# One issue list, 130 of 2459 operations in another place: an S4D convolution and a linear attention on one core

## The chip, the cores and the metric

The kernel runs on one core of one Trainium2 chip. The metric is the device time of one execution in microseconds; three executions of the kernel before the change took 543.41, 543.82 and 544.84 us, median 543.82. Engine names as the profile has them: PE is TensorE (PEld its weight loads), DVE is VectorE, ACT is ScalarE, POOL is GpSimd, SP is the engine that here issues all DMAs (SPq its queue).

## The reference

Two independent halves, concatenated along the last axis; 2048 positions, 576 channels, all float32.

```python
def _A_ref(u, log_A_real, A_imag, C_real, C_imag, log_dt, D_skip):
    dt = jnp.exp(log_dt)
    A = -jnp.exp(log_A_real) + 1j * A_imag
    C = (C_real + 1j * C_imag) * dt[:, None]
    P = jnp.exp((A * dt[:, None])[:, :, None] * pos[None, None, :])   # 576 x 128 x 2048
    K = 2.0 * jnp.einsum("dn,dnl->dl", C, P).real
    y = irfft(rfft(u_t, 2L) * rfft(K, 2L), 2L)[:, :, :L]              # a causal convolution
    return y.transpose(0, 2, 1) + u * D_skip[None, None, :]

def _B_ref(x, wqkv, w_phi, wo):                                       # 32 heads of 18
    q, k, v = split(x @ wqkv)
    pq, pk = q @ w_phi, k @ w_phi                                     # per head
    phi_q = concat([softmax(pq), softmax(-pq)]); phi_k = the same of pk
    kv = einsum("bhsf,bhsd->bhfd", phi_k, v); z = phi_k summed over s
    o = (phi_q @ kv) / (phi_q @ z + 1e-6)
    return o.reshape(B, S, D) @ wo
```

## The kernel before

The convolution is done as a two-stage Fourier transform by matmuls. Its parts, by the names in the program: `u` (16 units, the first transform stage of the input, stored to DRAM), `par` and `mags` (the parameters: steps and magnitudes), `group` (18 units, each of which builds a piece of the long kernel K: phases on GpSimd in integers, a sine on ScalarE, a rotation by matmuls `g0`, ScalarE copies `g2` at L811, VectorE multiplications `g3` at L815 to L820, and a reduction by 64 small matmuls `g4`), `kfirst` (4 units, the first stage of the transform of K), `product` (16 units: load spectra `ff` and `ub`, matmuls `p1` and `p2`, the complex product, the inverse stage `p4`, a store), and `last` (16 units: load, `l1` a matmul with `w1`, a copy to `ot`, four stores to the output at L979). The attention has `fold` (weights of wqkv and w_phi multiplied), 16 `key` tiles of 128 positions (projection, two softmaxes, `k4`: the sum of phi_k times v), `kv`, and 16 `query` tiles (projection, softmaxes, product with kv, division, product with wo, a store at L589). Large matmuls go in two float32 halves (`vh`, `vl`, `wh`, `wl`).

All of it is made first as a list of 2459 operations numbered in the order in which the body calls them, and then issued in the order of one long string, `ORDER`. No scheduler runs: each engine has one queue in program order, and what is in front in the string is in front in its engine's queue. An operation starts when its queue has come to it and its semaphores are there. A word of `ORDER` is a number, with `x` for the other of two permitted engines, `@` and digits for the PSUM bank or banks of its result (8 banks), and `:n` for n zero matmuls put on TensorE ahead of it, written into the bank that the operation itself will write:

```python
            word, _, fill = word.partition(":")
            word, _, at = word.partition("@")
            k = int(word.rstrip("x"))
...
            for _ in range(fill):
                self.matmul(t[0:cols, 0:n], self.zero.t[0:rows, 0:cols], ...)
```

Buffers in SBUF belong to tags with a number of copies that are used in turn (`e`, `x9`, `ot` and `ac` have 3, `cs` and `ub` 5, `ff`, `zo`, `zi` 2, `small` 7), so an operation that writes a buffer also waits until the last user of that copy is done. SP issues its DMAs in the string's order; the ninth waits until the first has landed, and so on: eight are under way at most.

The operations that the prediction names:

| number | what it is | engine before |
|---|---|---|
| 298 | key tile 12: maximum minus e (softmax, L310) | VectorE |
| 278, 279 | key tile 11: minimum (L437), then its subtraction | VectorE, GpSimd |
| 80, 81 | key tile 1: maximum (L434), e minus it (L314) | VectorE |
| 1140, 1141, 1432 | par: phase arithmetic (L314, L734) | VectorE |
| 173, 174 | key tile 6: low half of x (L310) | VectorE, GpSimd |
| 303, 305 | key tile 12: clearing of v (L487); `k4` | GpSimd, TensorE |
| 386, 366, 396 | fold and kv: a copy of a weight, an output copy; a fold product | VectorE, VectorE, TensorE |
| 1034, 1035, 1036 | u 8: matmul, its two copies (L300) | TensorE, ScalarE, VectorE |
| 1444, 1470, 1520, 1519, 1943 | group: `g0` (1444, 1519, 1520, 1943), `g4` (1470) | TensorE |
| 463, 464, 465, 466 | query tile 1: minimum, subtraction, exponential, sum | VectorE, VectorE, ScalarE, GpSimd |
| 428 | query tile 0: e minus maximum | VectorE |
| 1540, 1543, 1546 | group 8: copy (L811), multiplication (L816), `g4` | ScalarE, VectorE, TensorE |
| 2305, 2263, 2221; 2278 | products 14, 12, 10: load of `ff`; product 12's `p4` | SP; TensorE |
| 2033, 2111 | products 1, 5: load of `ub` | SP |
| 2380, 2385, 2387, 2350, 2353 | last 4, 5, 5, 0, 0: output store (L979) | SP |
| 2424, 2431, 2438 | last 11, 12, 13: load (L966) | SP |
| 2432, 2439 | last 12, 13: `l1` | TensorE |
| 2434, 2443, 2449, 2455 | last 12, 13, 14, 15: output store (L979) | SP |
| 880, 917 | query tiles 12, 13: output store (L589) | SP |
| 773; 544, 1338, 1471, 1801 | query 10: low half of x; four copies out of PSUM | VectorE |
| 1932, 2014, 2020 | a copy, product 0's multiplication (L938), a copy | ScalarE, GpSimd, ScalarE |

Of the kernel before, what the change touches and what calls it, by code (L numbers as in the profile page):

```python
# [1000 lines left out]
113 114 84 1196 1018 1007 75 1038 1205 1230 1197 1198 211 1182 1179 280 1185 1186 281 1231 282 179@0 177@2 1142 176 116@6 117 325 115 175 1206 85 180
181 182 1207 1208 183x 86 1143 283x 286 1190@52 1232 1233 1234 120 121 87x 1187@3 1218 1189@67 1235 1237 1238 1239 326 122 1221 1188 178 327 1209 1404
212 189 1211 328x 123x 88 118@2 330@0 90 119 213x 124 1210 1212 1214 1213 1191@67 184 129 1215 185 1220 188 1240 1144 1241 1216@5 214 1242 216@2 215
1145 1146 1269 91 1243 128 1236 1223 186 306 1268 187x 1224 1219 1222 92 1217 93 1405 1270 1271 331@6 219 220 94 332 1100 329 221 222 125 190 126 1419
# [67 lines left out]
968 969 872@60 2418@2 2431 940@1 873 874 2448 2456 2457 2449 875 876 941 944 970 971@6 975@0 878@4 972 945 2419 942 946@17 2458 947 973@6 2451 2450  # L1072
877 879 976x 974x 948 2410 2455 2420 2422 2421 2423 2432@2 2439@0 2440 949 2403 2411@4 880 980@6 981 982 2424 950 2433 977@0 2444 951@2 978 2441 2436
979 983@10 2412 2442 984 2443 985 2437 986 2404@6 2435 2415 2434 2405x 2425@4 2426 2414 952 2416 2413 2409 2408 2407 2406 2428 2430 953 954 2427 2429
987 988@6 989 990 991
"""


# [16 lines left out]
```

## Time and profile before

| | |
|---|---|
| runs | 543.41, 543.82, 544.84 us |
| the profiled execution | 545.11 us, of which 543.3 us from the first to the last instruction |
| TensorE busy | 521.5 us (96%), granted clock 0.998 |
| VectorE, ScalarE, GpSimd busy | 455.9 (84%), 382.1 (70%), 328.8 (61%) us |
| DMA | 107.01 MB, mean 197 GB/s |
| zero matmuls | 118 |

In the timeline's rows stand the start, the length, the engine, the line, the operation, output and inputs and, in brackets, how long the engine had been idle ahead of it and what released it. Rows of neighbouring equal instructions are joined (x2, x64).

### The profile page before, as it was taken

How to read it: one execution, taken by the hardware profiler on the slowest of the kernel's cores; microseconds unless marked ns; L12 is line 12 of the kernel's file. 1: busy time of each engine (PE TensorE's matmuls, PEld its weight loads, DVE VectorE, ACT ScalarE, POOL GpSimd, SP SyncE). 2: the span in 40 equal slices, each digit the busy share in tenths (PEclk: the TensorE clock that was granted, in tenths of full speed). 3: DMA queues.
4: the chain of work that ended last, by engine and by line, in shares of the span. 5: the costliest groups of instructions: out<-in, count | busy, mean ns of one | idle time of the engine just before them, and what ended most of it. 6: DMA issues, size and time to landing. Idle time of an engine off the chain costs nothing.

```text
span 543.3 us, 19242 instructions
## 1 busy us (share of the span) xinstructions
PE 521.5 (96%) x8192; PEld 435.9 (80%) x8192; DVE 455.9 (84%) x716; ACT 382.1 (70%) x555; POOL 328.8 (61%) x456
## 2 busy tenths in 40 slices
PE   8999999999999989999999999999899999999995
PEld 7999899888888767888878666766689877776984
DVE  7999899898868889999989996999974889787641
ACT  4868798798559799889689977989733444343332
POOL 1173885958777775982758998997433617434300
PEclk9999999999999999999999999999999999999999
DMA  8936711244245678246664588756458789998785
GB/s 235 326 105 195 281 45 31 101 139 134 89 139 190 207 241 294 83 128 196 229 205 118 153 265 250 241 180 194 131 173 271 234 281 293 287 281 260 265 252 157
DMA packets 86163, 107.01 MB, mean 197 GB/s; under 512 B 5698, under 2 KB 70338, under 8 KB 86078
## 3 DMA queue, kind: packets, MB, share of 16 engines
q1 hardware_dynamic: 86078, 105.79, 61.5%
q8 instruction: 64, 1.05, 0.8%
q14 instruction: 21, 0.17, 0.1%
HBM read 61.22 MB, written 44.54 MB: 195 GB/s over the span
## 4 chain that ended last, share of the span: by engine, by line
PE 69%; DVE 13%; DMA 7%; ACT 4%; issue 3%; SPq 2%; POOL 1%; DVEq 0%; ACTq 0%; POOLq 0%
PE psum L295 63%; PE psum L549 3%; DMA ff<-in_ff_dram 2%; DMA dram<-zi 2%; PE psum L237 2%; DVE ac L314 1%; DVE cs L816 1%; SPq L979 1%; PE psum L577 1%; DMA cs<-dram 1%; DVE e L310 1%; DMA ub<-dram 1%; DVE e L314 1%; DVE small L434 1%; DVE small L437 1%
## 5 line engine op out<-in xcount | busy, mean ns | idle before, releaser
L295 PE MATMUL psum<-vh,x 128*128 128x288 f32 x576 | 123.6, 301 | 0.5 <-ACT ks L300 0.5
L295 PE MATMUL psum<-wh,x 128*128 128x288 f32 x576 | 124.1, 302 | 0.0
L757 POOL TENSOR_TENSOR cs<-cs,pi 128x32 int32<-128x32 int32 (+4 forms) x180 | 108.5, 608 | 8.0
L295 PEld LDWEIGHTS psum<-wh,x 128*128 128x128 f32 x576 | 94.1, 188 | 7.7 <-issue 4.2
L295 PEld LDWEIGHTS psum<-vh,x 128*128 128x128 f32 x576 | 94.0, 188 | 5.4 <-issue 3.2
L295 PE MATMUL psum<-vl,x 128*128 128x288 f32 x320 | 93.8, 295 | 0.0
L295 PE MATMUL psum<-wl,x 128*128 128x288 f32 x320 | 93.7, 295 | 0.0
L811 ACT ACTIVATE psum<-psum 128x512 f32<-128x512 f32 x108 | 59.9, 588 | 15.4 <-PE psum L295 14.9
L295 PEld LDWEIGHTS psum<-vl,x 128*128 128x128 f32 x320 | 60.2, 188 | 0.0
L295 PEld LDWEIGHTS psum<-wl,x 128*128 128x128 f32 x320 | 60.2, 188 | 0.0
L310 POOL TENSOR_TENSOR x<-zo,x 64x128 fp32r<-64x128 f32 (+1 forms) x30 | 25.4, 848 | 46.3 <-ACT x L394 35.1
L310 POOL TENSOR_TENSOR e<-e,small 128x1152 f32<-128x1152 f32 (+1 forms) x24 | 41.2, 1720 | 14.5 <-DVE small L450 7.8
L815 DVE TENSOR_TENSOR cs<-psum,cs 128x1024 f32<-128x1024 f32 x36 | 43.6, 1212 | 3.7 <-ACT psum L811 3.6
L310 POOL TENSOR_TENSOR e<-small,e 128x576 f32<-128x576 f32 x26 | 30.6, 1177 | 25.4 <-DVE small L437 23.6
L816 DVE TENSOR_TENSOR cs<-psum,cs 128x1024 f32<-128x1024 f32 x36 | 43.6, 1214 | 1.4 <-PE psum L295 1.3
L295 PE MATMUL psum<-ub,ff 64*32 64x288 f32 x1024 | 40.0, 410 | 4.3 <-DMA ff<-in_ff_dram 1.9
L295 PEld LDWEIGHTS psum<-kvb,fT 126*128 126x128 f32 (+1 forms) x320 | 38.3, 188 | 7.2 <-issue 2.9
L295 PEld LDWEIGHTS psum<-cs 128*32 128x32 f32 x2304 | 34.1, 110 | 11.2 <-issue 2.9
L295 PE MATMUL psum<-cs 128*32 128x64 f32 x2304 | 40.0, 220 | 2.6 <-DVE cs L816 0.9
L295 PE MATMUL psum<-kvb,fT 126*128 126x133 f32 (+1 forms) x320 | 41.6, 280 | 0.1
L440 ACT ACTIVATE e<-e 128x1152 f32<-128x1152 f32 x32 | 37.0, 1164 | 2.7 <-POOL e L310 1.3
L781 ACT ACTIVATE cs<-cs 128x1040 f32<-128x1040 int32 x36 | 38.3, 1064 | 0.6 <-POOL cs L776 0.4
(156 smaller groups left out, 1115.2 us busy)
## 6 DMA issues: line engine op xcount, KB each, us to landing
dram<-zi SPq DMA_DIRECT2D x32, 576.0 KB
ub<-dram SPq DMA_DIRECT2D x64, 288.0 KB
dram<-zo SPq DMA_DIRECT2D x32, 288.0 KB
zo<-in_xT_dram SPq DMA_DIRECT2D x24, 320.0 KB
zi<-dram SPq DMA_DIRECT2D x12, 576.0 KB
ub<-in_u_dram SPq DMA_DIRECT2D x16, 288.0 KB
xd<-x SPq DMA_DIRECT2D x8, 576.0 KB
x<-xd SPq DMA_DIRECT2D x8, 576.0 KB
```

The lines of the kernel that those rows point to most:

```text
L237: self.matmul(t[0:cols, 0:n], self.zero.t[0:rows, 0:cols], self.data.t[0:rows].bitcast(BF16)[:, 0:n], start=not o[13], stop=not o[13], ski ...
L295: pe.matmul(o, l, r, start=start, stop=stop, skip_group_check=skip)
L310: op(eng, [c_dve(n[0]) if e == "dve" else c_pool(n[1]) for e in eng], lambda e: (dve if e == "dve" else pool).tensor_tensor(dst(), a(), b( ...
L314: op(eng, c_dve(n) if eng == "dve" else c_pool(n), lambda: e.tensor_tensor(dst(), a(), b(), op=alu), r=r, w=w, with_=with_, lock=eng == "p ...
L434: op("dve", c_dve(D), lambda: dve.tensor_reduce(two(top.t), v(), axis=AX.X, op=ALU.max, negate=True), r=[p], w=[top])
L440: op("act", c_act(1152) + 40, lambda: act.activation(e.t, e.t, AF.Exp), r=[e], w=[e], table="exp")
L549: pe.transpose(tp.t[0:m, j - j0, :], e.t[:, sign, 7 * g:7 * g + GRP[g], :].rearrange("p h f -> p (h f)"), ident.t)
L757: op("pool", c_pool(2 * n * W), lambda n=n, j=j: pool.tensor_tensor(x()[:, :, :, n:2 * n], x()[:, :, :, 0:n], pi.t[:, j:j + 2, gs].bitcast ...
L781: act.activation(cs.t[:, 1], cs.t[:, 1].bitcast(I32), AF.Sin, scale=TURN)
L811: op("act", c_act(512), lambda b=b: act.activation(b.t, b.t, AF.Exp), r=[b], w=[b], table="exp")
L815: op("dve", c_dve(64 * W), lambda: dve.tensor_tensor(F(), both(M.t), F(), op=ALU.mult), r=[M, cs], w=[cs])
L816: op("dve", c_dve(64 * W), lambda: dve.tensor_tensor(E.t[:, :, :, 32:64], both(up.t), cs.t[:, :, :, 0:32], op=ALU.mult), r=[up, cs], w=[E])
```

## The change

Only the string `ORDER` differs. Buffers, operations and their arithmetic are the same. 130 operations stand in another place, nearly all a few words from where they were; 2033 and 2111 go back over fourteen and eight of SP's DMAs, 2424 forward over some fifteen, 2393 over ten, 853 back behind several of GpSimd's. Eleven change the engine: 298, 464 and 773 from VectorE to GpSimd; 544, 1338, 1471 and 1801 from VectorE to ScalarE; 1035, 1932 and 2020 from ScalarE to VectorE; 2014 from GpSimd to VectorE. Zero matmuls: 749, 792, 1044, 1520 and 2278 get two, 1444 and 1943 four, 1993 two in place of three. Some 20 operations write another PSUM bank. The parts of the string with the larger changes (words of `ORDER`, shortened to those places):

```diff
-1200 1163 293 273@6 272 357 66 67 73x 1159 1164 1160 1065 1088 298x 1089 50@4 299 358 1090 1168 74 1165 70 304 359 1166 1167 77@2 300 276 1139 1401
-301 277 1402 362 172 173x 1169 1170 1192 302 76 274@0 1140 275 80 278 1141 1403 1091 1148 1147 279 1149 1150 174 303 1193 1201 1151@56 1172 111 1098
+1200 1163 293 66 273@6 272 357 67 73x 360 1159 1164 1160 358 298 1065 1088 1089 50@4 299 1090 1168 74 1165 70 304 1166 1167 77@2 300 276 359 1139 1401
+301 277 1402 362 172 1169 1170 1192 1193 302 76 274@0 278 1403 1140 275 80 81 1141 173x 1091 1148 1147 279 1149 1150 174 303 1201 1151@56 111 1098
...
-1524 1525 1526 366 1036x 1529 1531 1532 386 1443@54 1527 1528 1533 1534 1462 1463 1009@06 1464 1035 1011 1444@23 403@6 1466 1467 402 1535 1445@54 1465
-1472 1010 406 1468 404 394 1473 1043 1537 387 458 1469 1470@2 1474 396@0 395 1536 399 408 1475 1037 405 407 1471x 1476 388@6 1478 1477 1361 1362 389
+1522 1523 1524 1525 386 1526 366 1036x 1529 1531 1532 1443@54 1527 1528 1533 1534 1462 1463 1009@06 1011 1464 1035x 1444@23:4 403@6 1466 1467 402 1535
+1445@54 1465 1472 1010 406 1468 404 394 1473 1043 1537 396@0 387 458 1469 1470@2 1474 395 1536 399 408 1475 1037 405 407 1471 1476 388@6 1478 1477
...
-994@62 398 995x 372x 996x 1012 415 459@0 364 365 1429 460 369x 374x 1430 373x 370x 375 1431 997 461 462 1432 426@6 425 1538 463 1376 416 417 1433
-1044@24 464x 1434 1435 1688 376 377 1520@01 427 428 1377 1519@67 1539 1046 1045x 155 1436 1541 429 526 465 492 418 1542 1014@24:8 430 1540 1545 1544
+371@5 368x 1013 994@62 398 995x 372x 1012 415 459@0 364 374x 365 996x 1429 460 369x 1430 373x 370x 375 1431 997 461 462 426@6 425 1538 463 1432 1376
+416 417 1433 1044@14:2 1434 464 1435 1688 376 377 427 428 1377 1519@67 1539 1046 1045x 1520@01:2 155 1436 1541 1540 429 526 465 492 418 1542 1014@42:8
...
+956 957x 958x 898 2229 858 767 902 843 2353 2322 2221 2323 2228 2277 924 2385 2350 2362@4 2226@0 2324 2352 925 926 2224@2 2363x 2232@4 2325 2396 768
...
-934@2 935 938@5 2241 963 2402 870 2401 2400 939 867 964 965 966 871 868 936@6 915 916 2445 2452 937x 2446@2 2447 2417 2453@4 967 2454x 2438 943@7 917
-968 969 872@60 2418@2 2431 940@1 873 874 2448 2456 2457 2449 875 876 941 944 970 971@6 975@0 878@4 972 945 2419 942 946@17 2458 947 973@6 2451 2450
-877 879 976x 974x 948 2410 2455 2420 2422 2421 2423 2432@2 2439@0 2440 949 2403 2411@4 880 980@6 981 982 2424 950 2433 977@0 2444 951@2 978 2441 2436
+2417 2453@4 967 2454x 2438 2424 943@7 917 968 969 872@60 2418@2 2431 940@1 873 2449 874 2448 2456 2457 875 876 941 944 970 971@6 975@0 878@4 972 945
+2419 942 946@17 2458 947 973@6 2451 2450 877 2455 879 976x 974x 948 2410 2439@0 2420 2422 2421 2423 2432@2 2440 949 2403 2411@4 880 2443 980@6 981 982
```

More of the change, by code (lines that the diff above doesn't have):

```diff
@@ L1001 @@
[L1001 to L1004, printed above, removed]
@@ L1073 @@
[L1073 to L1075 removed]
+0 1 2 4 1104 3 1097 1093 68 1094 5 1096 1154 1105 1107 34 6 1092 1108 1109 51 1095 27 7@0:49 20 1106 1110 1111 1112 1113 1114 1115 8 35@2 1199 1137 11
+28@4 29 52 12 1116 1120 9 53x 30 36 10 54 13 22@6 32 37 1003 21 1117 39 992 1118 31 1119 40 15@0 14 1074 23 33 38 1121 1063 344 18 25 16 345 24
@@ new lines @@
+2000@6 2001 1844 1733 2123 1837 1810 588 589 2124@24 2125 2126 1845x 2002@6 2006@0 2008@4 1945 1846x 2003 2007 2009 2012 2010 2011 1818 624@6 2014x
+625 2127 1947 626x 1803@20 2130 1805x 1811@46 1847 1812x 1804 1813 2013 2015@20 636 2132 1826@6 2129 2138 2128 637 2137 2016 1827 1948 1949 2135@4
+2133@6 2090 1950 1952 1953 2017 1954 2018x 2136 2141@4 2022x 1955 2134 2020x 2142 2019 1956 2139@6 2021 525 1828@23 590@0 1848 2089 2140 1829@45 1849
+2095 1851 1852 1830@67 1850 1853 1957 1958 1951 591 663@2 2023 1959 1854 1857 1860 2144 1960x 638 2143 1855@4 592x 1858 664 1859 1915 639 1862 1961
@@ new lines @@
+2088 1914 1916 1863 1861 1917 665 666 667 2093@0 2091@6 2092 1856 1864@5 1814 2094 2096 2097@6 1918 640 1919 2024 696 1920 2099@2 697 1865x 627
+2145@04 2098 668 1907 1942@67 1962 2100 2075 1908 2146 2069 1963 643@2 669 698 1909 1943@34:4 1964 1965 641@5 642 645@6 699 1971 2147 700@0 2102 644
+1944@52 1966 1967 1968 1974 1910 1973 2101 1969@7 646 701 1806 1911 1972 1922 1970 670 1912 671 1913 1976 1921 2067 2148 2149 2068 1977 672 1975 593
+2150 2074 673 1877 674 2103@62 2104 702 1978@4 703 1876 2070@2 1870 1869 2033 2025 2072@0 647@5 2026 1878 2027 1979x 2071x 2073x 2105 2107 650@4 1923
@@ new lines @@
+706 707 810 2040@02 688 1930 1929 689 1941x 2200 690 691 1931@4 1932x 1980 1993@64:2 2041 773 2042 1995x 1994 1981@20 1989@64 1982x 2044 1983x 2043
+774@2 708 1996 775 1990 733 709 710 711x 776 734 735 736 777 1984 778 779 1991 692@0 1985@62 1987 811@4 714@2 2045 715 1986x 812 1992 813 712@3 1988
+844 713x 716@6 780 2368 2180 693 717 781 718@7 721@6 782 814 738@2 2369@4 719 694 722 720 783 784 2179 2175@0 881 2370 845 846 847 723 2183@6 2181@4
+737 2389 2176 724@01 815 816 2182 725 2184 726 727 739 2185 728 817 882 883x 849@4 848 785x 850 2207 661 730@6 786@0 787 851 2372 2201 695 884 2202
@@ new lines @@
+2373 2250 2186 852 729 790@1 731 2187 788@0 818 819 820 2208 2375 2189 2188 2374 789 2203@4 2371 791x 732 2205@6 2204 2390@0 2243 2206 2211@4 740
+2209@2 2212 2391 2190@60 2191 795@5 792@4:2 2307 2210 2192 821 2244 2193x 2196 822x 823@2:6 2194 2195 2242 2213x 2197 796 2249 2247@0 793 824 797 794
+2214x 2245@6 2376@2 2248 2246 2253@0 2347 2377 2251@4 2215@62 2198 2199 2254 2252 2393 741 2327 885@0 2216 798@23 742 2328 799 2217 2218x 825@4 827@5
+2326 800 801 826x 2333 886 2329@6 2334 828x 802 2219 887 2330 2394 2331@4 2332 743 2335@2 2337@6 2220 888 2382 2336 2256 2255 2257@04 889 2258 2285
@@ new lines @@
+832@2 744 890 829@3 2338 2286 803@4 2259 2339x 745 2284 833 830 834 2383@6 891 831 2384 2289@0 2392 2287@2 2260 2291 892 746 2290x 835@67 893 836 853
+837 2288 804 747 838 839 2261 2395 2340 2341@02 2292 2293@6 805 2295@4 748 2262 2342 2361 753@2 751@3 2343 2306 2380 2313 2296 752 841@0 2294 2305
+749@3:2 754x 2308@6 750 2381 2310@4 2309x 2312 2316@2 2311 2344 2314@6 2317 758@5 2345 2265 2378 2298 755@4 2297 2315 756 759 894 757 895 760 896x
+2346 2299@26 806 918 919 920x 761@45 762 840 921 2270 763 2264 899@4 2387 2379 2300 764 2319 2348@6 2301 2318 842 2263 2266@2 900x 2267 2268@0 765
@@ L1076 @@
+2407 2406 2428 2430 953 954 2427 2429 987 988@6 989 990 991
 """
```

119 lines of the change are left out of this document (51 added, 68 removed).

## The prediction

> **What bounds the kernel.** I read the page's busy times and its chain first, then busy time by stretch, then what TensorE waited for, then the timeline where a wait stood beside a moved operation.
>
> ```profile
> PE 521.5 (96%) x8192; PEld 435.9 (80%) x8192; DVE 455.9 (84%) x716; ACT 382.1 (70%) x555; POOL 328.8 (61%) x456
> ...
> PE 69%; DVE 13%; DMA 7%; ACT 4%; issue 3%; SPq 2%; POOL 1%; DVEq 0%; ACTq 0%; POOLq 0%
> ```
> ```profile
> 28.00:56.00 28.00, 27.30 (x329) 25.26 (x330) 27.85 (x39) 22.16 (x28) 15.38 (x24) 1.00 0.52 165
> ...
> 180.00:220.00 40.00, 35.72 (x599) 30.01 (x600) 34.24 (x61) 36.27 (x52) 27.70 (x41) 1.00 0.81 264
> ...
> 442.00:500.00 58.00, 56.00 (x920) 42.05 (x907) 46.54 (x71) 23.63 (x38) 28.30 (x21) 1.00 0.93 290
> 500.00:543.30 43.30, 37.33 (x406) 32.97 (x390) 18.37 (x40) 14.48 (x25) 6.14 (x5) 0.98 0.69 219
> ```
>
> TensorE is busy 521.5 of 543.3 us and nothing of its real work changes, so a reordering can only win what it stands idle, or lose by more of it. By stretch (columns: stretch, its length, then PE, PEld, DVE, ACT, POOL busy, clock, DMA share, GB/s) VectorE has no gap at 28 to 56, TensorE idles 4.3 us at 180 to 220 and 6.0 us in the tail, and the DMA engines are 93% busy at 442 to 500. So I price four places and a residue; elsewhere the moves mostly swap neighbours whose inputs are there in either order, and I put them at zero with the engines' queues as cover. If that cover is thin, the waits quoted below show what one slip costs: 0.25 to 1.2 us each.
>
> **Part 1, at 55 us: operation 298 (key tile 12's subtraction) goes from VectorE to GpSimd; 278 is put ahead of 1140 and 80, and 173 behind 1141.**
>
> ```profile
> 41.59 1.02 DVE L310 TENSOR_TENSOR e<-small,e 128x576 f32<-128x576 f32 x1
> ...
> 51.64 0.54 DVE L314 TENSOR_TENSOR pi<-pi,ot 128x384 f32<-128x384 f32 x1
> 52.10 0.74 DVE L434 TENSOR_REDUCE small<-psum 128x32 f32<-128x576 f32 x1
> 52.77 0.73 DVE L437 TENSOR_REDUCE small<-e 128x32 f32<-128x576 f32 x1
> ...
> 40.40 0.72 POOL L310 TENSOR_TENSOR x<-zo,x 64x128 fp32r<-64x128 f32 x1 [3.12 <-ACT x L394]
> ...
> 53.66 1.41 POOL L310 TENSOR_TENSOR e<-small,e 128x576 f32<-128x576 f32 x1 [8.76 <-DVE small L437]
> ...
> 55.66 0.16 POOL L487 MEMSET v<- 128x32 f32 x1
> ...
> 54.77 0.18 PEld L295 LDWEIGHTS psum<-sel,mg 64*128 64x128 f32 x1 [0.54 <-DVE e L314]
> 55.87 0.75 PE L295 MATMUL psum<-e,v 128*19 128x36 f32 x64 [0.60 <-POOL v L487]
> ```
>
> TensorE waits 0.54 us (81, VectorE, which also frees a bank) and 0.60 us (303, the GpSimd memset). GpSimd stood idle 8.76 us for 278 (the L437 row), then ran 279, 174 and 303 in a row. Without 298 VectorE is 1.02 us ahead; 278 also passes 0.54 + 0.74, so 279 starts some 2.5 us earlier and ends near 52.6. Then 174 needs 173, which now stands behind 1141: near 53.8; 303 follows at about 54.5. TensorE would come to its product at 55.87 - 0.60 - 0.54 = 54.7. Both waits go: 0.54 + 0.60 = 1.1 us. 298 itself fits in GpSimd's gap of 3.12 us ahead of 40.40. Late next would be 303 itself, with 0.2 us to spare; for 173 only 174 waits. Bounds: 0 (another wait takes over) to -1.1.
>
> **A rule on GpSimd against the rows.**
>
> ```profile
> 39.43 1.36 DVE L310 TENSOR_TENSOR e<-e,small 128x1152 f32<-128x1152 f32 x1
> ...
> 44.34 1.70 DVE L310 TENSOR_TENSOR e<-e,small 128x1152 f32<-128x1152 f32 x1
> ...
> 207.25 2.29 POOL L383 TENSOR_TENSOR vl<-e,vh 128x960 fp32r<-128x960 f32 x1 [2.27 <-ACT vh L382]
> ...
> 208.70 1.25 DVE L314 TENSOR_TENSOR pi<-pi,ot 128x384 f32<-128x384 f32 x1
> ```
>
> The same VectorE product took 1.36 and 1.70 us; the same addition took 0.54 alone and 1.25 at 208.70, ending 0.41 after GpSimd's 2.29 us operation ended. So a GpSimd tensor operation holds up some VectorE ones beside it. The Trainium skill (SBUF — State Buffer, "Who interferes with whom") says that VectorE and GpSimd share one port pair under an exclusive lock, so that the later one is blocked for the whole instruction; these rows agree. By that rule moving work to GpSimd is no gain where a VectorE operation with two inputs in SBUF comes due during it. By it the sum stays as below if the moved operations meet no such operation, and loses parts 1 and 3 if they do. From the rows alone: 298 takes 1.0 to 1.4 us on GpSimd; from the idle of 3.12 us ahead of 40.40 (37.3) it ends by 38.7, before the product at 39.43, and 464 (below) stands beside operations that read PSUM. I take no loss; the other outcome is rival B.
>
> **Part 2, at 190 us.** 386 passes 366 and 1036 on VectorE; 1035 goes from ScalarE to VectorE; 396 goes ahead of 1470; 1444 gets 4 zero matmuls.
>
> ```profile
> 192.03 0.49 PE L295 MATMUL psum<-sel,mg 64*128 64x512 f32 x2 [1.18 <-ACT zi L300]
> ...
> 194.63 0.58 PE L295 MATMUL psum<-cs 128*32 128x64 f32 x25 [0.25 <-DVE cs L820]
> ...
> 193.90 0.68 DVE L820 SCALAR_TENSOR_TENSOR cs<-psum,cs 128x512 f32<-128x512 f32 x1
> ...
> 191.03 1.23 DVE L815 TENSOR_TENSOR cs<-psum,cs 128x1024 f32<-128x1024 f32 x1 [1.28 <-ACT psum L811]
> ```
>
> The wait of 1.18 us shrinks, since VectorE empties 1035's bank earlier, and the 4 zero matmuls lie in it. But the next wait does not move: 1470 (194.63) waits for the VectorE run from 191.03 to 193.90 + 0.68 = 194.58, which starts with a ScalarE operation that none of this hastens. So time won at 192 is waited for at 194.6, and what remains is that 396 now lies inside that wait: at least the 0.25 us which the row shows, at most its own length (some 0.5, an estimate by the 0.49 of 192.03). I take -0.35; bounds 0 and -1.2, the wait gone whole.
>
> **Part 3, at 213 to 218 us.** 464 goes to GpSimd, 463 passes 1432 (the 1.25 us row), 1540 passes 465 on ScalarE, 1519 stands ahead of 1520.
>
> ```profile
> 210.81 0.74 DVE L310 TENSOR_TENSOR e<-small,e 128x576 f32<-128x576 f32 x1
> ...
> 213.12 0.50 PE L295 MATMUL psum<-sel,mg 64*128 64x512 f32 x2 [0.80 <-DVE e L314]
> 213.79 1.03 PE L237 MATMUL psum<-ident,zero 64*128 64x256 bf16 x8 [0.16 <-DVE zi L300]
> ...
> 215.74 0.81 PE L237 MATMUL psum<-ident,zero 64*128 64x256 bf16 x6
> ...
> 218.16 1.10 PE L295 MATMUL psum<-cs 128*32 128x64 f32 x64 [0.89 <-DVE cs L816]
> ```
>
> 464's 0.74 us leaves VectorE, but the two operations behind it must still wait for TensorE, so 428 ends only some 0.5 us earlier. 1543, which releases 1546 (218.16), starts when 1540 and VectorE are done; 1540 now comes a ScalarE exponential earlier, so VectorE's own 0.5 to 0.6 us count, and the 0.89 us wait shrinks by that. The zero matmuls between keep their length. I take -0.6; bounds 0 and -1.7 (0.80 + 0.89). Who waits for ScalarE's 465, now behind 1540: GpSimd's 466, 0.2 us later, with slack.
>
> **Part 4, zero matmuls and loads.** One zero matmul costs (1.03 - 0.81) / 2 = 0.11 us, all 17 together 1.9.
>
> ```profile
> 358.13 0.49 PE L295 MATMUL psum<-sel,mg 64*128 64x512 f32 x2
> ...
> 493.57 1.23 PE L295 MATMUL psum<-ac,ff 32*64 32x288 f32 x32
> ...
> 491.95 0.48 PE L295 MATMUL psum<-ub,ff 64*32 64x288 f32 x8 [0.49 <-DMA ff<-in_ff_dram]
> ...
> 478.99 2.18 PE L295 MATMUL psum<-ub,ff 64*32 64x288 f32 x64 [0.94 <-DMA ff<-in_ff_dram]
> ...
> 486.18 0.58 SPq L979 DMA_DIRECT2D out_dram<-ot  x1
> 486.86 0.54 SPq L895 DMA_DIRECT2D ff<-in_ff_dram  x1
> ```
>
> Eleven stand where TensorE waits anyway (ahead of 1444 the 1.18, ahead of 1519 and 1520 the 0.80, and ahead of loads). The 4 ahead of 1943 (358.13) and the 2 ahead of 2278 (493.57) have no wait before them: 6 x 0.11 = +0.65; bounds -0.1 (one fewer at 1993) and +1.9. On SP's queue 2385, 2387 and 2350 (0.58 us each) no longer stand ahead of the load 2221 (486.86) but 2353 does: it is issued over 1 us earlier, and its 0.49 us wait goes; I take -0.6 with what PEld lost there, bounds 0 and -0.8. 2380 and 2387 now stand ahead of the loads 2305 and 2263 instead: up to 0.58 each; these loads wait for a free buffer before they issue, so I take +0.2 each, +0.4; bounds 0 and +1.2. SP's other moves (2033 by 24 us, 2111 by 21) are of loads used 12 and 6 us after their new place: zero. So do the other engine changes (773 to GpSimd; 544, 1338, 1471, 1801 to ScalarE; 1932, 2014, 2020 to VectorE) and the exchanged PSUM banks: one operation of about a microsecond or less each, in queues with room in the same stretch; without that room each would cost its own length, and B and C hold that.
>
> **Part 5, the tail.** Load 2424 moves from behind 880 to behind 2438; 2443, 2449, 2455 and 2434 pass neighbours; 2439 passes 2432 on TensorE.
>
> ```profile
> 508.02 0.57 SPq L966 DMA_DIRECT2D cs<-dram  x1
> 514.04 0.34 SPq L589 DMA_DIRECT2D out_dram<-ot  x1
> ...
> 520.67 3.18 SPq L979 DMA_DIRECT2D out_dram<-ot  x5
> ...
> 525.55 12.56 SPq L979 DMA_DIRECT2D out_dram<-ot  x18
> ```
> ```profile
> 525.03 6.00 DMA cs<-dram
> ...
> 531.09 0.57 SPq L979
> ```
>
> The chain of the tail is SP issuing stores of 0.6 us, broken by one load: issued at 525.03, landed at 531.03, and only then the next store goes. SP has an idle gap from 508.59 to 514.04 where the load now goes. Out of the chain fall its 0.42 + 0.10 us of issue and the gap before 531.09: 18 stores at 0.64 (3.18 for 5) would take 11.5, the row has 12.56, so 1.1. Together -1.6; I take -1.5, since the last store needs a ScalarE copy that follows the stores. Bounds -0.4 (the issue alone; another wait fills the gap) and -2.1 (2439 earlier adds 0.5). The load's bytes now delay 917 and 2431, wanted at 523.6, nine microseconds later.
>
> **Sum.** -1.1 - 0.35 - 0.6 + 0.65 - 0.6 + 0.4 - 1.5 = -3.1. The profiled execution took 545.11 us (span 543.3 and 1.8 around it), 1.3 above the median of 543.82; so 542.0 there and 540.7 by the median. All lower ends: 543.8 - 7.0 = 536.8; all upper: 546.5.
>
> **Rivals.** A, slower: stores ahead of loads. In the stretch at 93% DMA share TensorE waits for ff loads near 441, 468, 479 and 492; if the reordered stores cost each of them two issues of 0.58 in line, 1.2 us, that is +4.7 in place of the -0.6 + 0.4 above: 540.7 + 4.9 = 545.6. It decides from about +4.5, or less if parts 1 to 3 fail with it. For it: the 93%; against: 2305 and 2263 wait for a buffer anyway, and 2221 has fewer stores ahead of it than now. B: the gains on TensorE don't arrive. GpSimd's moved operations meet VectorE's, by the lock as above, parts 1 and 3 go, and the tail alone wins: 543.8 - 0.35 + 0.45 - 1.5 = 542.4. For it: each stretch has another wait within 20 us; against: those waits hang on TensorE's own results and shift with it. C: more is won; the small moves I put at zero give another 2 to 3 us of the 22 that TensorE idles: 538.
>
> **Chances.** The sum as it stands 0.50, B 0.23, A 0.14, C 0.13. This kernel's measurement can tell 0.3%, 1.6 us, from no change. Faster by over 0.3%: the sum (0.46 of it) and C (0.13), with a little of B: 0.61. Within it: 0.23. Slower: 0.16. Range 537.4 to 545.0, which leaves out most of A and a little of C.
>
> **What would show it.** Part 1: the product at 55.87 starts near 54.7, with no GpSimd wait. Part 2: the 1.18 wait gone, the one on L820 longer. Part 3: 218.16's wait under 0.4. Part 4: the row like 358.13 preceded by four zero matmuls with idle 0; the wait on ff at 491.95 gone, those at 468 and 479 no longer than 1.2. Part 5: no DMA piece of cs in the tail's chain, SP's stores without a gap from 525 to the end. Wrong, if TensorE's busy time plus waits is unchanged by 500 us, or if the tail's chain shows a new landing in 2424's place.

## The result and the profile after

After takes 537.96 us in the median (537.79 to 540.34), before 543.62 in the runs beside it: a ratio of 0.9885, 95% interval 0.9852 to 0.9919, so 1.15% faster. The forecast was 540.7 from a median of 543.82, 0.57% faster. Direction and range hold; the gain is twice the one forecast.

The page of after, its first part and the first line of its chain:

```profile
PE 519.3 (97%) x8209; PEld 434.7 (81%) x8209; DVE 450.8 (84%) x713; ACT 381.2 (71%) x556; POOL 329.8 (62%) x458
...
PE 81%; DVE 6%; DMA 4%; ACT 3%; issue 3%; POOL 2%; SPq 1%; ACTq 0%; POOLq 0%; DVEq 0%
```

The same stretches as before, the tail cut at after's own end (stretch, length, PE, PEld, DVE, ACT, POOL busy, clock, DMA share, GB/s):

```profile
28.00:56.00 28.00, 28.00 (x383) 26.30 (x382) 27.13 (x40) 21.63 (x28) 19.04 (x31) 1.00 0.50 162
180.00:220.00 40.00, 37.55 (x618) 31.86 (x617) 34.47 (x64) 35.84 (x52) 29.20 (x47) 1.00 0.72 241
442.00:500.00 58.00, 56.93 (x867) 43.52 (x866) 45.75 (x73) 23.84 (x39) 29.91 (x23) 1.00 0.87 277
500.00:536.10 36.10, 30.73 (x331) 26.57 (x329) 13.59 (x32) 11.42 (x20) 4.80 (x4) 0.99 0.73 234
```

TensorE has no gap left at 28 to 56 and 2.4 us instead of 4.3 at 180 to 220. In the tail it still stands idle 5.4 us (before 6.0): the place with the largest forecast changed least. TensorE's share of the chain went from 69 to 81%, VectorE's from 13 to 6 and DMA's from 7 to 4. TensorE's instructions at the priced places, after:

```profile
54.33 0.73 PE L295 MATMUL psum<-sel,mg 64*128 64x512 f32 x4
54.99 0.75 PE L295 MATMUL psum<-e,v 128*19 128x36 f32 x64
...
191.81 1.10 PE L295 MATMUL psum<-cs 128*32 128x64 f32 x64 [0.29 <-DVE cs L820]
...
209.54 0.50 PE L295 MATMUL psum<-sel,mg 64*128 64x512 f32 x2 [0.41 <-DVE e L314]
...
214.32 1.10 PE L295 MATMUL psum<-cs 128*32 128x64 f32 x64
```

Neither wait of part 1 is there, and the product starts at 54.99. 1470 (191.81) still waits for L820, as forecast. 1546 (214.32) waits for nothing, and 0.41 is left of the 0.80 at 1519.

### The profile page after: what moved, and what is told of

Its sections match the earlier page's. It is cut to its first block, busy times and chain, and to the rows that moved or that the text cites. A ratio compares the mean times of both kernels' runs of the same rounds, so it can differ in the third digit from the quotient of the medians.

```text
span 536.1 us, 19272 instructions
## 1 busy us (share of the span) xinstructions
PE 519.3 (97%) x8209; PEld 434.7 (81%) x8209; DVE 450.8 (84%) x713; ACT 381.2 (71%) x556; POOL 329.8 (62%) x458
## 4 chain that ended last, share of the span: by engine, by line
PE 81%; DVE 6%; DMA 4%; ACT 3%; issue 3%; POOL 2%; SPq 1%; ACTq 0%; POOLq 0%; DVEq 0%
PE psum L295 74%; PE psum L549 3%; PE psum L237 2%; DMA ff<-in_ff_dram 2%; DVE cs L816 2%; PE psum L577 1%; DMA zi<-dram 1%; POOL cs L757 1%; DMA x<-xd 1%; DVE cs L820 1%; SPq L979 1%; DVE cs L818 1%; ACT psum L811 1%; POOL ac L310 1%; DVE ac L314 0%
## 5 line engine op out<-in xcount | busy, mean ns | idle before, releaser
L811 ACT ACTIVATE psum<-psum 128x512 f32<-128x512 f32 x108 | 59.6, 586 | 14.2 <-PE psum L295 13.7
L310 POOL TENSOR_TENSOR e<-small,e 128x576 f32<-128x576 f32 x28 | 33.2, 1186 | 24.4 <-DVE small L437 21.8
L300 ACT ACTIVATE zi<-psum 128x576 f32<-128x576 f32 x41 | 25.8, 649 | 19.6 <-PE psum L295 14.1
```

What stands on the lines that cost most here:

```text
L300: op(("act", "dve"), (c_act(n), c_dve(n)), lambda e: act.activation(dst(), src(), AF.Copy) if e == "act" else dve.tensor_copy(dst(), src() ...
L310: op(eng, [c_dve(n[0]) if e == "dve" else c_pool(n[1]) for e in eng], lambda e: (dve if e == "dve" else pool).tensor_tensor(dst(), a(), b( ...
L811: op("act", c_act(512), lambda b=b: act.activation(b.t, b.t, AF.Exp), r=[b], w=[b], table="exp")
```

## Where the time went, place by place

One number for a whole run hides which place moved, and single runs of one kernel differ by 2.5 us (after, 537.79 to 540.34), and by 6 us among the runs of before beside e1 (543.15 to 549.51). So I followed TensorE's operations: the end of an operation in before's trace, less its end in another kernel's trace, is that kernel's lead at this point, and the growth of the lead between two operations is what the stretch between won. Positions are before's; the marks are the operations 15, 79, 198, 1263, 1304, 170, 395, 1546, 2154, 1815, 2000, 2139, 909 and the end. All kernels but after are experiments below: e13 is after once more, e8 after without its new zero matmuls, e14 without four TensorE moves, e15 without six load moves, e16 without both and without the exchange of 1258 and 337. The last column is the range over the kernels whose order in that stretch is before's: what chance alone does.

| stretch (us) | after | e13 | e8 | e14 | e15 | e16 | order as before |
|---|---|---|---|---|---|---|---|
| 13.8 to 58.7 (part 1) | 1.39 | 1.31 | 0.33 | 0.32 | 0.70 | 1.37 | 0.00 to 0.15 |
| to 114.5 | 0.64 | 0.64 | 0.63 | 0.00 | 0.61 | 0.00 | -0.02 to 0.01 |
| to 116.7 | 0.62 | 0.62 | 0.62 | 0.62 | 0.62 | 0.00 | 0.00 to 0.02 |
| to 137.5 | 0.33 | 0.31 | 0.10 | -0.33 | -0.12 | 0.56 | 0.05 to 0.54 |
| to 187.6 | 0.34 | 0.29 | 0.34 | 0.02 | 0.23 | 0.02 | -0.13 to 0.04 |
| to 197 (part 2) | 0.23 | 0.22 | 0.23 | 0.22 | 0.22 | 0.22 | -1.19 to 0.01 |
| to 219.3 (part 3) | 0.78 | 0.43 | 1.02 | 0.71 | 0.71 | 1.02 | -0.24 to 0.01 |
| to 282.6 | 1.34 | 1.09 | 1.08 | 1.07 | 1.35 | 1.20 | 0.27 to 0.96 |
| to 324.8 | 0.75 | 0.76 | 0.75 | 0.75 | 0.74 | 0.75 | -0.67 to 0.01 |
| to 327.2 | 1.02 | 0.98 | 1.01 | 1.02 | -0.15 | -0.57 | -0.74 to 0.12 |
| to 341.0 | -1.02 | -0.78 | 0.00 | -1.17 | 0.01 | 0.01 | 0.00 to 0.01 |
| to 502.0 (part 4's loads) | 0.86 | 1.14 | 1.20 | 1.50 | 1.90 | 0.53 | -0.32 to 1.04 |
| to the end (part 5) | 0.40 | -2.35 | 0.87 | -1.81 | 0.48 | 0.29 | -0.94 to 0.27 |

Each row is worked out in the same way; for 1263 the rows stand under e10: it ends at 115.62 + 1.10 before and 113.47 + 1.10 after, a lead of 2.15; the operation ahead of it has 114.39 - 112.86 = 1.53, so 0.62 is won between the two.

## The experiments

In e1 to e7 a part of the list of after stands in an `ORDER` that is otherwise before's; the numbers are places in the list.

**e1, the tail alone.**

```diff
-ORDER places 2304 to 2459: before's
+ORDER places 2304 to 2459: after's
```


> Only the last part of the issue list is the changed one (everything from 915 and 2424 on: the load 2424 early, the stores of the last units exchanged, 2439 ahead of 2432); the rest is the list of before. Theory S (the gain is spread over many small moves, the tail is a small part): 0.4 to 0.8 us faster than before, since comparing the two traces TensorE is 6.5 us ahead at 525 us and 7.2 at the end. Theory C (the priced places carry it, the tail as I priced it): 1.5 us faster, bounds 0.4 to 2.1.

Measured: 544.23 us, ratio 0.9967 (0.9942 to 0.9992), -1.8 us with an interval of 1.4 either way. Its trace wins only 0.20 from 502 to the end. The time fits the forecast's 1.5, the trace does not; e13 below decides.

**e2 and e5, parts 1 to 3.** In e2 the two lists meet inside u unit 4, and one half of this unit's result is overwritten, so its output differs from before's; e5 ends at a place where the unit is whole.

```diff
-ORDER places 0 to 300, 797 to 961 (e2) or 1170 (e5): before's
+ORDER places 0 to 300, 797 to 961 (e2) or 1170 (e5): after's
```


> Only the stretches 0 to 63 us and 187 to 221 us are in the changed order (parts 1, 2 and 3 of the prediction, 298, 464 and 1035 on their new engines); the rest is the list of before. Theory S: 2.0 to 2.4 us faster (the two traces differ by 0.9 at 57 us, and by 1.0 to 1.4 more between 187 and 219). Theory C: 2.05 us faster, as the prediction priced these parts. Both agree here; a gain under 1 us would say that the time won there is waited for later.

> As e2_parts123, but with the changed order up to 257 us, so that the PSUM banks of the two lists fit where they join (in e2 and e4 the lists joined at 219 us, and one half of u unit 4's result is overwritten there; their outputs differ from the reference's in that, and the bank waits cost some 0.8 us in e2 and 1.4 us in e4 after the join). Theory S: 2.5 to 3.5 us faster than before (2.0 of e2 and what the join cost). Theory C: 2.05 us faster.

Measured: e2 0.9963 (0.9936 to 0.9990), e5 0.9948 (0.9922 to 0.9973): -2.0 and -2.8 us against a forecast of 2.05. In the trace part 3 wins 0.97 in e5 and 0.65 in e2, part 1 1.39 in e2 and only 0.16 in e5, for a reason that stands under the next heading.

**e3, places 300 to 797, which the forecast put at zero.**

```diff
-ORDER places 300 to 797: before's
+ORDER places 300 to 797: after's
```


> Only the moves between 69 and 187 us are the changed ones (key tiles' products 90, 150, 267 behind their neighbours, 1187 and 1190 exchanged, 1258 behind 337 and 1257, store 1348 early, 1338 on ScalarE), which the prediction put at zero. Theory S: 1.0 to 1.6 us faster (the two traces drift apart by 0.7 at 72 to 84 us, 0.6 at 116, 0.3 at 137). Theory C: within 0.3 us of before.

Measured: 0.9966 (0.9941 to 0.9990), -1.85 us. The places are not worth zero.

**e4 and e6, the middle.** e4 starts where e2 ends and overwrites the same half of u unit 4; e6 starts at the clean place.

```diff
-ORDER places 961 (e4) or 1170 (e6) to 1914: before's
+ORDER places 961 (e4) or 1170 (e6) to 1914: after's
```


> Only the moves between 219 and 414 us are the changed ones (load 2152 ahead of 2153 and 2151 and 1608 early near 275, loads 1998, 1999, 2111, 2117, 2033 elsewhere, the four zero matmuls ahead of 1943, 681 ahead of 2036, 1867 behind 1905); the prediction put them at zero but for the zero matmuls, +0.4. Theory S: 1.5 to 2.5 us faster, 1.3 of it at 282 us, where the wait for the load 2152 is gone in the changed kernel's trace. Theory C: 0.4 us slower to equal.

> Only the moves between 257 and 414 us are the changed ones: e4 without the join. Theory S: 1.5 to 2.0 us faster. Theory C: 0 to 0.4 us slower, the four zero matmuls ahead of 1943 uncovered.

Measured: e4 0.9990 (0.9962 to 1.0018), e6 0.9971 (0.9943 to 0.9999). Both win 0.72 from 282.6 to 324.8 and 1.02 at 327; e4 loses 1.03 ahead of that at its seam.

**e7, the loads and stores of 434 to 501** (part 4 without the zero matmuls ahead of 1943; six others are in it).

```diff
-ORDER places 1914 to 2304: before's
+ORDER places 1914 to 2304: after's
```


> Only the moves between 434 and 501 us are the changed ones: stores and loads on SP's queue (2380, 2387, 2353 earlier, 2385, 2350, 2379 later, 2222 earlier), 795 ahead of 792, 862 ahead of 2236, 853 later, six zero matmuls. Theory S: 0.5 to 1.0 us faster, since the two traces come 0.8 us closer to the end over this stretch. Theory C: my terms, -0.6 + 0.4 + 0.2, equal within 0.3 us. Rival A of the prediction: slower.

Measured: 0.9993 (0.9966 to 1.0019): no change that can be told.

**e8, after without its new zero matmuls.**

```diff
-1444@23:4 ... 1044@14:2 ... 1520@01:2 ... 1943@34:4 ... 792@4:2 ... 749@3:2 ... 2278@60:2
+1444@23 ... 1044@14 ... 1520@01 ... 1943@34 ... 792@4 ... 749@3 ... 2278@60
```


> The changed kernel without its 17 new zero matmuls (749, 792, 1044, 1444, 1520, 1943, 2278 with none, 1993 as in the changed kernel). If those at 1943 and 2278 are uncovered, as the prediction has it, this is 0.65 us faster than the changed kernel, 6.3 us faster than before; near 351 and 488 us its trace gains 0.44 and 0.22. Rival: the wait behind them takes the time back, and it equals the changed kernel, 5.7 us faster than before.

Measured: 538.65 us, 0.9881 (0.9842 to 0.9920), after's own. In the time the zero matmuls cost nothing that can be told, but the interval is 2 us either way. In the traces the four at 1943 do cost something: TensorE loses 0.34 us there in after and nothing in e8, and after has 0.16 of it back by 375.

**e9 and e10: the places of e3, split.** Between operations of different tile mode (rows by columns that a matmul uses) the distance from one start to the next is longer than inside an operation. Over the boundaries in the traces of before and after the median excess is 0.09 us from a 128 by 128 operation into a smaller mode, 0.14 out of 128 by 32, and 0.3 to 0.4 out of the modes of 64 and 32 rows. Before's 240 changes of mode add up to 46 to 50 us, by how the overlapping row halves of a 64 by 128 operation are counted; after's 234 are 1.0 us less either way. The Trainium skill (TensorEngine Tiling (Array Packing), "Key Properties") says that changing the tiling mode drains TensorE; the trace agrees, and the sizes are from the trace. e9 has only the four moves that save changes, e10 all others of e3.

```diff
-1190@52 1232 1233 1234 120 121 87x 1187@3
+1187@3 1190@52 1232 1233 1234 120 121 87x
-90 119 213x 124 1210 1212 1214 1213 1191@67
+119 213x 124 1210 1212 1214 1213 1191@67 90
-1481@67 264x 1502 267
+264x 267 1481@67 1502
-150 385 159 1348 1517@5 384 169x
+385 159 1348 1517@5 384 169x 150
```


> The kernel before with four TensorE operations moved and nothing else (a vector operation goes along with one of them): 1187 ahead of 1190, 90 behind 1191, 267 ahead of 1481, 150 behind 1517. Each move puts operations of the same tile mode beside each other, so TensorE changes its tile mode eight times less. Theory M (a change of mode costs 0.09 us into a mode of fewer rows or columns, 0.14 out of 128x32, 0.33 out of the modes of 64 and 32 rows, by the gaps between instructions in the traces of before and after): 46.41 us of changes become 45.07, so 1.3 us faster, ratio about 0.9975, and in the trace the same work at 187 us ends 1.2 to 1.5 us earlier than before's, most of it by 84 us (two of the four), the rest at 172 to 186. Rival R (the gain of these stretches is from the moves on ScalarE and GpSimd and the store 1348): no change of the time, under 0.3 us at 187.

> The other half of the early moves outside the priced places: after's list in places 300 to 797 with the same four TensorE operations left where before has them, so the changes of tile mode cost 46.41 us as before. Theory M: nothing, 1.000 within 0.002, shift at 187 us under 0.3 us. Rival R: these moves carry the gain of the early stretch, 1.3 to 1.9 us, ratio about 0.9970.

Measured: e9 0.9999 (0.9979 to 1.0018), e10 1.0006 (0.9983 to 1.0029). In time neither half gives what e3 gives. The timeline of TensorE shows why for e9, first before, then after, then e9:

```profile
71.42 0.75 PE L295 MATMUL psum<-e,v 128*19 128x36 f32 x64
72.11 0.50 PE L295 MATMUL psum<-sel,mg 64*128 64x512 f32 x2
72.53 1.10 PE L295 MATMUL psum<-cs 128*32 128x64 f32 x64
73.57 0.51 PE L295 MATMUL psum<-sel,mg 64*128 64x512 f32 x2
```
```profile
70.53 0.72 PE L295 MATMUL psum<-e,v 128*19 128x36 f32 x62
...
71.08 1.10 PE L295 MATMUL psum<-cs 128*32 128x64 f32 x63
72.11 0.74 PE L295 MATMUL psum<-sel,mg 64*128 64x512 f32 x4
```
```profile
177.41 1.10 PE L295 MATMUL psum<-cs 128*32 128x64 f32 x64 [0.79 <-DVE cs L818]
```

The same four operations take 73.57 + 0.51 - 71.42 = 2.66 us before and 72.11 + 0.74 - 70.53 = 2.32 after, 0.34 less, from nothing but their order. In e9 that is won too, but moving 1481 behind 267 makes its group's VectorE work late, and 1508 waits 0.79 us for it. In after and in e3, where ScalarE and VectorE were reordered along with it, that wait is 0.27. e10 shows the other piece, the exchange of 1258 and 337 on ScalarE (L811 and L440, both exponentials): before, then after.

```profile
115.62 1.10 PE L295 MATMUL psum<-cs 128*32 128x64 f32 x64 [0.48 <-ACT ks L300]
...
105.07 0.58 ACT L811 ACTIVATE psum<-psum 128x512 f32<-128x512 f32 x1 [0.90 <-PE psum L295]
105.56 1.16 ACT L440 ACTIVATE e<-e 128x1152 f32<-128x1152 f32 x1
...
115.21 0.36 ACT L300 ACTIVATE ks<-psum 128x256 f32<-128x256 f32 x1
```
```profile
113.47 1.10 PE L295 MATMUL psum<-cs 128*32 128x64 f32 x64
...
102.63 1.17 ACT L440 ACTIVATE e<-e 128x1152 f32<-128x1152 f32 x1
103.70 1.06 ACT L811 ACTIVATE psum<-psum 128x512 f32<-128x512 f32 x2
...
112.76 0.36 ACT L300 ACTIVATE ks<-psum 128x256 f32<-128x256 f32 x1
```

In before 1258 stood ahead of 337 and made ScalarE's whole queue wait 0.90 us for its product. In after 337 runs in this gap, everything behind it on ScalarE comes earlier, the copy ks (L300) too, and TensorE's wait of 0.48 for that copy is gone. In e16, with the exchange undone, ScalarE waits 0.91 at this place again.

**e11, six loads alone.**

```diff
-2153 2151 1628 ... 2152 ... 1722
+1628 ... 2152 ... 1722 2153 2151
-2111 1636 ... 2060 ... 2117 2005 ... 1834
+1636 ... 2060 2111 ... 2005 ... 1834 2117
-1997 1998 ... 2066 1999
+1998 ... 1997 ... 1999 2066
```


> The kernel before with only six loads moved in SyncE's order: 2153 and 2151 behind 2152, 2111 and 2117 later, 1998 and 1999 earlier. Theory L (the stretch 240 to 330 gained by what TensorE waited for loads there): the wait for 2152 (1.18 to 1.46 us at 275 to 282) and the wait of operation 2000 for 1999 (1.0 us at 325) go, so in the trace 1.3 us are won at 282 and 1.0 at 327; part of it is given back in the next waits, so the whole time is 0.8 to 2 us shorter, ratio 0.9963 to 0.9985. Rival (these waits are a matter of when the store 1032 lands, which differs from kernel to kernel): the same gain at 282 as other kernels with this load order unchanged had, but no gain at 327, and a ratio of 0.998 to 1.000.

Measured: 542.86 us, 0.9970 (0.9950 to 0.9991). The trace wins 1.01 at 327; at 282 it wins 0.59, which kernels with before's order also have (0.27 to 0.96). So 1998 and 1999 count and 2152 is not shown to. Operation 2000 in before, in after, and in e15, where the loads are back:

```profile
325.46 0.68 PE L295 MATMUL psum<-ub,ff 64*32 64x288 f32 x4
326.49 0.71 PE L295 MATMUL psum<-ub,ff 64*32 64x288 f32 x12 [0.35 <-DMA ub<-dram]
```
```profile
319.53 0.72 PE L295 MATMUL psum<-ub,ff 64*32 64x288 f32 x16
```
```profile
320.54 0.68 PE L295 MATMUL psum<-ub,ff 64*32 64x288 f32 x4
321.71 0.71 PE L295 MATMUL psum<-ub,ff 64*32 64x288 f32 x12 [0.50 <-DMA ub<-dram]
```

**e12, more moves of the mode kind.** 2230 takes over the PSUM banks of product 10's first result before that is read, so part of product 10 is changed.

```diff
 (on e8)
+643@2 behind 641@5, 343 behind 1263@5, 2230@2 behind 2232@4
```


> A version meant to beat both: after without its 17 new zero matmuls, and with three more TensorE operations moved beside others of their tile mode (643 behind 641, 343 behind 1263, 2230 behind 2232). Theory M: changes of mode cost 44.31 instead of 45.41 us, and 643 no longer waits 1.05 us for VectorE, so 1.0 to 2.0 us faster than after, about 536.5 us, ratio to before 0.985 to 0.9865. Rival (the TensorE time saved there becomes a wait for VectorE and ScalarE, since 343 delays two products by 0.66 us and 2230 one by 0.44 us that others wait for): 538 us, ratio 0.988 to 0.990.

Measured: 539.42 us, 0.9909 (0.9880 to 0.9937): no better than after. 343 ahead of two products makes TensorE wait 0.78 us for a ScalarE copy at 118, more than the change of mode saves. The rival is right.

**e13 to e16, after once more and with moves undone**, on one chip. e13 has after's list.

```diff
 e14: 1187@3 behind 87x, 90 ahead of 119, 1481@67 ahead of 264x, 150 ahead of 385
 e15: 2153 2151 ahead of 1628, 2111 behind 1635, 2117 ahead of 2005, 1998 behind 1997, 1999 behind 2066
 e16: both, and 1258 ahead of 337
```


> After once more, as the measure for the three that follow on the same chip: ratio to before 0.987 to 0.991.

> After with the four TensorE moves undone (1187, 90, 1481, 150 back where before has them), so its changes of tile mode cost 46.75 us instead of 45.41. If the mode moves pay because the rest of the change keeps the vector work ahead of them: 0.7 to 1.3 us slower than after (ratio to before 0.0013 to 0.0024 higher), and in the trace 0.2 to 0.35 us lost at each of the four places. If they pay nothing, as e9's time has it: within 0.4 us of after.

> After with the six loads of 2153, 2151, 2111, 2117, 1998 and 1999 put back to their places of before. If they carry the middle of the excess, as e11 has it: 1.0 to 2.0 us slower than after (0.0018 to 0.0037 in the ratio), with TensorE's wait for 2152 back at 275 to 280 (1.2 to 1.5 us) and operation 2000's stop for 1999 back at 320 (1.0 us). If those waits are only a matter of when a store lands: within 0.5 us of after.

> After with the four TensorE moves, the six loads and ScalarE's exchange of 1258 and 337 all undone: what is left is mostly the priced parts. If the excess over the forecast is these moves, 2.0 to 3.5 us slower than after, which is the forecast's own 540.7 on this chip's scale (ratio to before 0.9925 to 0.995). If the priced parts were worth more than forecast: within 1 us of after (ratio under 0.991).

Measured: e13 0.9904 (0.9875 to 0.9933), e14 0.9914 (0.9887 to 0.9941), e15 0.9895 (0.9871 to 0.9920), e16 0.9919 (0.9894 to 0.9945). In time nothing is told apart; e16's 2.0 to 3.5 us came out as 0.8 us with intervals of some 1.5 either way on both. In the table each piece shows at its place: 0.6 us to 114.5 in every kernel with the four moves and 0.00 in both without, and 0.2 to 0.3 to 187.6 against 0.02; 0.62 at 116.7 and 0.00 in e16; 1.0 at 327 and none in e15 and e16. e15's zero in time has its reason in the row below that one: at 341 after, e13 and e14 lose 0.8 to 1.2 again, ahead of the last two of the 32 matmuls of operations 2141 and 2139, and e15 and e16 do not.

```profile
332.77 1.26 PE L295 MATMUL psum<-ub,ff 64*32 64x288 f32 x30 [0.28 <-ACT ac L300]
334.39 0.67 PE L295 MATMUL psum<-ub,ff 64*32 64x288 f32 x2 [0.36 <-issue]
```

These are after's rows; in e8 all 32 run in 1.29 us. The stop at 2139 is there only in kernels with both the early loads and the zero matmuls, and the profile names no releaser. Stops of this kind also stand elsewhere, in operation 1479 for one, in before and in after:

```profile
200.54 0.41 PE L295 MATMUL psum<-cs 128*32 128x64 f32 x11 [0.27 <-issue]
```
```profile
197.43 0.43 PE L295 MATMUL psum<-cs 128*32 128x64 f32 x15 [0.40 <-issue]
```

After has four zero matmuls more ahead of this operation, and its stop comes four matmuls earlier in it: counted over all of TensorE's matmuls it is at the same number. This speaks for a stop that goes by the count and not by the operation. What it is, and why some executions have none there, is open.

**e17 and e18, one load of the tail earlier**, meant to beat both.

```diff
 (e17 on after, e18 on e8)
-2431 ... 2449 ... 2455 ... 2410
+2431 2410 ... 2449 ... 2455
```


> After with one load moved: 2410 (cs of the last stage's unit 9) directly behind load 2431, ahead of the eight stores that stand between them. Theory T (in some executions SyncE stands at the store 2455 until load 2431 lands, 2410 behind it is issued 2 us later, and TensorE waits 2.0 to 2.2 us for it): 2410 is issued near 507.6 and lands by 515, TensorE has no wait for a DMA between 515 and 531, and the median is 0.5 to 2 us under that of after on this chip's scale, ratio 0.985 to 0.9885. Rival (the tail is bound by the number of stores and the earlier load only takes their bandwidth: another load, 2403, or the stores' end, is late instead): 0.989 to 0.992, with the wait moved to another operation after 520.

> The version meant to beat both: after without its 17 new zero matmuls and with 2410 directly behind 2431. Theory T: as the other, ratio 0.9845 to 0.988. In the trace no stop of TensorE of 0.8 to 1.2 us at the end of operation 2139 (near 334), which after has with its zero matmuls and the version without them did not. Rival: 0.988 to 0.992, as after.

Measured: 0.9925 (0.9901 to 0.9949) and 0.9925 (0.9895 to 0.9956). The rival is right: no wait for a DMA is left on TensorE there, and nothing is won. What grows instead in e17 is ScalarE's wait in the tail for output buffers, 12.8 us where it is 9.0 in after and 5.9 in before; that this is what binds is not shown by a run of its own:

```profile
ACT ot L300 <- DMA out_dram<-ot: 12.8, 6, 3.3
```

No version beat after.

## Why the prediction had the direction right and the sum wrong

**Part 1: right, but it depends on a race.** The mechanism is as forecast and 1.3 us come in some runs. In others another wait takes over, 0.92 to 0.94 us for a VectorE copy of v (L300). VectorE's addition and GpSimd's operation 279, first after, then e8:

```profile
51.11 0.56 DVE L314 TENSOR_TENSOR pi<-pi,ot 128x384 f32<-128x384 f32 x1
...
51.07 1.62 POOL L310 TENSOR_TENSOR e<-small,e 128x576 f32<-128x576 f32 x1 [5.98 <-DVE small L437]
```
```profile
50.83 1.54 DVE L314 TENSOR_TENSOR pi<-pi,ot 128x384 f32<-128x384 f32 x1
...
50.79 1.17 POOL L310 TENSOR_TENSOR e<-small,e 128x576 f32<-128x576 f32 x1 [5.78 <-DVE small L437]
...
56.38 0.41 PE L295 MATMUL psum<-vh,x 128*128 128x288 f32 x1 [0.92 <-DVE v L300]
```

Both start within 0.04 us, and one of them is held for most of the other's length. Where VectorE goes first, it takes 0.56 and GpSimd 1.62; where GpSimd goes first, VectorE takes 1.54 and TensorE waits. Seven kernels with this part went the first way (after, e2, e13, e15 to e18) and four the second (e5, e8, e12, e14). By the lock that the prediction cited from the Trainium skill (SBUF — State Buffer, "Who interferes with whom") one of two must wait; the trace agrees and shows that the order is not fixed. The mean of part 1 over the table's six is 0.90, against 1.1.

**Part 2: right, at two thirds of its size.** Every kernel with it wins 0.22 or 0.23 from 187.6 to 197, e2, e5, e14 and e16 too, which have none of the mode moves; kernels with before's order win nothing there. As forecast, the time won at 192 is waited for again: 1.01 us are won up to 1444, 1.00 of it is gone at 1470, which still waits 0.29 for L820, and what stays is 396 inside that wait, 0.22 against the 0.35 taken. Without its four zero matmuls (e8) 1444 ends another 0.43 earlier, and that is waited for at 1470 as well.

**Part 3: right.** 0.78 in the mean, 0.86 more than where the order is before's (mean -0.08), against 0.6.

**Part 4: its sum came out with the other sign, within the scatter.** Forecast +0.45. Of the 0.65 for uncovered zero matmuls the traces show 0.34 at 1943, half of it given back (e8 above); the 0.22 at 2278 is lost in larger differences there, and the time shows nothing. The wait for ff at 491.95 is gone, and TensorE's waits for ff are 0.9 us in all where they were 1.9; before, then after:

```profile
PE psum L295 <- DMA ff<-in_ff_dram: 1.9, 3, 0.9
```
```profile
PE psum L295 <- DMA ff<-in_ff_dram: 0.9, 2, 0.6
```

Products 14 and 12, whose loads are 2305 and 2263, wait for no load of ff after. From 341 to 502 after's six have 1.19 in the mean and kernels with before's order 0.39, but these alone scatter by 1.4. e7 alone measures nothing in time.

**Part 5: failed.** 2424 left the chain, as forecast, but the time did not follow. To the end, after's six have -0.35 us in the mean and kernels with before's order -0.28. The gap that the prediction put at 1.1 us did not go: the row of 18 stores, 12.56 us long before, is

```profile
517.08 0.53 SPq L966 DMA_DIRECT2D zi<-dram  x1
...
518.29 12.61 SPq L979 DMA_DIRECT2D out_dram<-ot  x18
```

after. The prediction read that the next store goes only when load 2424 has landed. In before seven stores went while it was under way, and the eighth transfer behind it, store 2415, stood until 531.09. In after load 2403, issued at 517.08, has come in its place: the eighth transfer behind it, store 2434, goes at 523.04 in place of 522.12, 0.92 us late. Once that is past, the chain of after goes through TensorE and ScalarE up to 525.00 and then through the stores. In e13, the same kernel, more is late: SP's own waits after, then in e13, and e13's TensorE.

```profile
SPq L979 <- DMA zi<-dram: 1.2, 2, 0.9
```
```profile
SPq L979 <- DMA zi<-dram: 3.6, 2, 2.9
```
```profile
520.08 0.72 PE L295 MATMUL psum<-cs,w 64*32 64x288 f32 x16 [2.15 <-DMA cs<-dram]
```

The two waits are those of store 2434 for load 2403 (the 0.9 in after) and of store 2455 for load 2431 (the 2.9 in e13). Load 2410 is queued behind 2455, was issued at 515.84 instead of 513.80, and TensorE waited 2.15 us. The prediction named the sign, a new landing in 2424's place. e17, where TensorE has no such wait, is no faster, so that something else would have held the tail; the output buffers are the likely one. e1's time (-1.8, at least -0.4) still speaks for some gain; how much stays open.

**The step that failed: "I put them at zero".** The moves without a price won about as much as the whole forecast. From 58.7 to 116.7 they win 0.63 + 0.62, from 137.5 to 187.6 another 0.33, to 324.8 0.75, and at 327 1.0, of which after gives 0.9 back by 341. From 219 to 282.6 it is 1.19 in the mean less 0.55 (mean of e1, e3, e7, e9, e10); this piece is the least certain, since e15 and e16 win it without the early loads, and e12 and e18, with after's order there, have only 0.33 and 0.76. That is some 3 us, rival C's size. Parts 1 to 4 give 0.9 + 0.2 + 0.9 and up to 0.8, the tail nothing. All in all 5 to 6 us, as measured (5.7 beside after, 5.2 in e13), by another sum than the one forecast: its largest single term was empty, and as much as its total lay where it had none. The pieces up to 187.6 and the loads at 327 are shown by undoing them, in the trace; the time of e14 to e16 is too coarse to confirm them. 324.8 is placed by e4 and e6 but not taken apart, and e12 loses its share there again at operation 2061. The cover that I named, the queues, was not there: 1258 held ScalarE's queue for 0.90 us and cost TensorE 0.48, and load 1999 cost it 1.0, the size that the prediction gave for a slip; after removes both.

Rival A's loads did not come late; of B the lock is real and took three quarters of part 1 (0.3 us won in place of 1.26, in the mean) in four kernels of eleven.

## What to carry to other kernels

On an engine that is 96% busy, count what its neighbours cost each other too: four moves that put operations of one tile mode together won some 0.3 us each in after without removing any wait; one of them lost it again in a wait of 0.27, and in e9, where the engines that feed it were not moved along, in one of 0.79. Price each exchange in a queue by whether the input of the one in front is there: "neighbours whose inputs are there" was wrong for 1258, which held back everything behind it for 0.90 us while 337 could have run. A transfer taken out of a queue that waits for the one eight before it can leave the wait in place, with another load. And follow the lead from operation to operation through several traces: there a piece of 0.6 us shows to 0.02 us where a dozen timed runs could not tell 1 us.

## What the runs showed of the hardware

A change of tile mode holds TensorE 0.09 us on the way from 128 by 128 into a smaller mode and 0.14 to 0.4 us on the way out, 46 to 50 us in a span of 543. Two operations on VectorE and GpSimd that come due 0.04 us apart may run in either order, at 0.56 and 1.62 us or at 1.54 and 1.17. A store can stand on SP's queue until the load eight transfers before has landed (2455 for 2431, until 513.18 in after and 515.22 in e13; 2434 for 2403, until 523.04 in after). A stop of TensorE without a releaser came at the same number in its list of matmuls in before and after (0.27 and 0.40 us in operation 1479), though not at the same matmul of the operation.
